# Token forms' hi copies moved behind, the output weights split earlier, and another order in the fold: one change to a fused attention and MLP kernel on one core

## The chip, the cores and the metric

The kernel runs on one core of a Trainium2 chip. The time is device time in microseconds (us) of one launch. The names in the profile: PE is TensorE's matmul, PEld its weight load, DVE VectorE, ACT ScalarE, POOL GpSimd, SP SyncE, whose queue issues nearly all DMAs. Each engine takes its instructions in the order in which they stand in its queue, and waits on semaphores where an operand or a buffer is not ready.

## The reference, cut to what matters

```python
def _A_ref(x, wqkv, w_phi, wo):                      # S=2048, D=640, H=32 heads of 20
    q, k, v = split_heads(x @ wqkv)
    pq, pk = einsum("bhsd,hdf->bhsf", q, w_phi), einsum("bhsd,hdf->bhsf", k, w_phi)
    phi_q = concat([softmax(pq), softmax(-pq)], -1)
    phi_k = concat([softmax(pk), softmax(-pk)], -1)
    kv, z = einsum("bhsf,bhsd->bhfd", phi_k, v), sum_s(phi_k)
    o = (phi_q @ kv) / (phi_q @ z + 1e-6)
    return merge_heads(o) @ wo
def _B_ref(x, w1, b1, w2, b2):                       # F=1728
    h = gelu(layernorm(x) @ w1 + b1)
    return h @ w2 + b2
xn = layernorm(x)
return x + _A_ref(xn, ...) + _B_ref(xn, ...)
```

All is float32. The kernel gets that precision from matmuls in a shorter format by splitting each operand exactly into a hi and a lo part: hi is a rounded copy (mostly on ACT), lo is the operand minus hi (on DVE or POOL). A product is then three matmuls, hi*hi, hi*lo and lo*hi (`mm3`).

## The kernel before, in words

The 2048 tokens are four blocks of 512 (b = 0 to 3), the 640 channels five chunks of 128 (c). The stages follow each other on TensorE:

1. **First MLP pass** (tokens of blocks 0 and 1). The 1728 hidden units are handled in pairs of chunks, g = 0 to 6. `Mlp.passes(g, b)` has two halves. The first makes the hidden values: for each of two chunks five groups of `mm3`, then gelu (L293, on ACT), hi (L60, ACT) and lo (L63, DVE). The second makes five output chunks (m) with two groups each, and DVE adds each to `acc` (L338). The second half of one pass stands on TensorE behind the first half of the next. The outputs use three PSUM banks in turn, so output m+3 cannot start until L338 has read output m.
2. **Attention features** (L1025, L1397, L1401 on TensorE): q, k and v for sixteen token tiles t, then softmax features on all engines, and the sums kv (L1138). Some products of pairs of tiles are done with seven block products in place of eight, which needs sums and differences of both operands: the forms.
3. **Second MLP pass** (blocks 2 and 3), with attention's second half beside it, then the output product with `wo`, in hi and lo parts that lie ready in the DRAM buffers `wo_dram`.

**What runs beside the first MLP pass.** A generator (`mlp.beside`) is advanced by one step at each tick. A tick is one `mm3` group on TensorE, three matmuls, and the order in which its steps and the pass's own instructions are written is the order in the queues of ACT, DVE and POOL. SP's queue is ordered by the scheduler. The generator is `prep()`, and beside it `turned_forms()`:

- `prep_fold`, the fold: products of `wqkv` and `w_phi` (L650 on TensorE), seven jobs of two units, ten ticks each. Each unit's product is split into hi (L738, ACT) and lo (L741, DVE), and its two PSUM banks are used again by the next job. Between them `more_stats` takes layernorm statistics of later tokens on DVE.
- `turned_forms`: forms of blocks 0 and 1. For block 1 ACT's own queue issues the stores (L932).
- The later tokens (blocks 2 and 3), driven by a list of events (tick, step). For each token tile (c, b): a load of `xq` from `xT`, `centred` (L797, POOL), `scaled` (L800, DVE), `hi` (L804, ACT), `lo` (L808, DVE) and two stores. For each pair of channel chunks, a cycle q: `form_sub`, four subtractions (L834, POOL); `form_hi`, two copies (L838, ACT); `form_lo` (L842, DVE) and their stores (L845). Then four `combine` subtractions (L820, POOL), each with its hi (L804), lo (L825) and a store of 512 KB (L826). Hi and lo of tiles and combinations lie in two buffers `t` in turn.
- Where the pass takes its next weights (`take`), two hi copies (L60, ACT) and two lo subtractions (L63, POOL) stand among these.
- At the end `raw_sums` prepares sums of the weights for attention's products. Steps that the ticks did not reach are written out in one go before g = 6's second pass.

**The order in attention** is found by a list scheduler at build time (`Plan.run`): each operation gets an assumed duration, times `LONGER` for all engines but TensorE, and each engine takes the operation that is due first. The rest follows in TensorE's order. The lo part of a k feature (L1090) goes to POOL or DVE, whichever the planner finds free. `plan_wo` puts the splitting of `wo` there: ten pieces of 128 x 320, from tile 4 on, each with a load (L1518, SP) into the buffer `r2`, a hi copy (L1521, ACT), a subtraction (L1524, POOL) and two stores (L1528). `r2` also holds weights of the second MLP pass, split there by L1550 (ACT) and L1551 (POOL). In the same queues v's hi and lo parts stand: L1119 (ACT) and L1124 (DVE). They free the PSUM bank of the projection.

Of the kernel before, what the change touches and what calls it, by code (L numbers as in the profile page):

```python
# [9 lines left out]
F32R = mybir.dt.float32r  # L10
AF = mybir.ActivationFunctionType
# [4 lines left out]
P = 128  # L16
S, D, F, H, DH = 2048, 640, 1728, 32, 20
KC = D // P
# [32 lines left out]
def tile_kernel(ctx: ExitStack, tc: tile.TileContext, x, xT, wkT, wqT, wv, wphi, wo, w1, b1, w2, b2,  # L51
# [671 lines left out]
    def prep_fold(batch, ts, done=None):  # L723
# [21 lines left out]
        for n, d in enumerate(done):  # L745
            yield from split_w(*d)
            for _ in range(3 + n):
                yield

    def more_stats():  # L750

        def tiles():
            xbs = {}
            for t in (*range(8, 16), None):
                if t is not None:
                    xbs[t] = gp.tile([P, 2, 512], F32, name="t").rearrange("p a c -> p (a c)")[:, :D]
                    with tc.issue_after(loads[1]):
                        nc.sync.dma_start(xbs[t], x[t * P:(t + 1) * P, :])
                if xbs and t != 8:
                    yield xbs.pop(min(xbs))  # L760
        yield from stats(range(8, 16), gp, tiles())
        for _ in range(2):
            yield
        yield from rows(2, 2, gp, mlp.px, 5)

    def prep():
        ahead = []
        more = more_stats()
        for i, job in enumerate(jobs):
            for k, _ in enumerate(prep_fold(job, ahead, None if i else first_done)):  # L770
                if k == 0 and i < 6:
                    ahead = raws(jobs[i + 1])
                if i > 0 and k % 3 == 1:
                    next(more, None)
                yield
# [72 lines left out]
        form_places = {2: temps[:4], 3: [z[:, o:o + 2 * P] for z in (spare[0], own["t"]) for o in (0, 2 * P)]}  # L848

        for n, step in enumerate(raw_sums(0, temps)):  # L850
            events.append((118 + 3 * n, len(events), step, ()))
        base = 8
        for q in range(3):
# [5 lines left out]
            if q < 2:  # L859
                for b, at, his, los in ((2, 14, (16, 18), (18, 20)), (3, 19, (21, 23), (23, 25))):  # L860
                    for i in range(4):
                        events.append((base + at + i, len(events), form_sub, (b, q, i)))
                    for i in range(2):
                        events.append((base + his[i], len(events), form_hi, (b, q, i)))
                        events.append((base + los[i], len(events), form_lo, (b, q, i)))
            base += 5 * len(tiles) + 5
            if q < 2:
# [42 lines left out]
    def turned_forms():  # L910

        for b, q in ((1, 1), (1, 0), (0, 0), (0, 1)):
# [9 lines left out]
            for i in range(2):  # L922
# [5 lines left out]
                yield 1  # L928
            yield 2
            for i, z in enumerate(parts):  # L930
# [3 lines left out]
            if (b, q) == (1, 0):  # L934
                yield 18

# [313 lines left out]

    LANDS, SOON, HURRY, AFTER, LONGER = 4.0, 0.9, -1.0, 10.0, 1.02
    plan = Plan()
# [125 lines left out]
    def plan_pair(t):  # L1378
# [70 lines left out]
        plan_wide(t, b1)  # L1449
        for n in range(t - 4, t - 2) if t > 2 else ():  # L1450
            plan_wo(n, at[t, 0])
        plan_kv(t - 1, c)
# [57 lines left out]
    def plan_wo(n, *after):  # L1510

        kc, cols = n // 2, slice(n % 2 * 320, n % 2 * 320 + 320)
        raw = {}

        def load():
            r = rp.tile([P, D], F32, name="r2")
            raw.update(lo=r[:, :320], hi=r[:, 320:])
            nc.sync.dma_start(raw["lo"], wo[kc * P:(kc + 1) * P, cols])  # L1518

# [6 lines left out]
        def store():  # L1526
            for w, wd in zip((raw["hi"], raw["lo"]), wo_dram):
                nc.sync.dma_start(wd[:, kc, cols], w)  # L1528

        a = plan.add("SP", 0.7, load, *after, *wo_done)  # L1530
        b = plan.add("ACT", 0.4, hi, a)
        c = plan.add("POOL", 1.0, lo, b)
        wo_done[:] = [plan.add("SP", 1.4, store, c)]
# [673 lines left out]
```

## Time and profile before

| | |
|---|---|
| median of 3 runs | 718.24 us (717.66 to 718.51) |
| the profiled execution | 718.39 us, span 716.6 us |
| busy PE, DVE, POOL, ACT | 97%, 77%, 71%, 53% of the span |
| first MLP pass | to about 224.7 us |
| attention features | 224.7 to 446.0 us |
| second MLP pass and output | from 446.0 us |
| mean granted TensorE clock | 0.99 |

A row of the timeline has the start in us, the duration, engine, line, operation, output<-input, shape and count. In brackets stands the idle time of that engine just before, and what released it. "SPq" and "ACTq" are DMA issues. The list of waits has, for each pair of waiter and releaser, the total, how many times, and the longest.

### The profile page before, as it was taken

What the parts mean: (1) busy time and instruction counts of PE and PEld (TensorE: products, weight loads), DVE (VectorE), ACT (ScalarE), POOL (GpSimd) and SP (SyncE); (2) the same over time, 40 slices, a digit from 0 to 9 for tenths busy, and PEclk for the clock granted to TensorE, in tenths of its full rate; (3) what the DMA queues carried; (4) which work ended last, traced back from release to release, by engine and by line L of the source; (5) the groups of instructions that cost most, each with busy time, mean ns of one, the idle gap of its engine ahead of it and who ended that gap; (6) DMA issues with size and microseconds to landing.
All of it is one profiled execution on the core that took longest, in us unless ns stands there. A gap on an engine that the chain in (4) does not pass through costs nothing.

```text
span 716.6 us, 9974 instructions
## 1 busy us (share of the span) xinstructions
PE 691.6 (97%) x3295; PEld 580.7 (81%) x3295; DVE 549.6 (77%) x915; ACT 376.8 (53%) x646; POOL 506.5 (71%) x389
## 2 busy tenths in 40 slices
PE   9999999788999999999999996999999999999998
PEld 7888888676788888888888784888888888888886
DVE  7869664777877889988989785958587687789783
ACT  6444744434433646545545353646667675659360
POOL 4707675749538678888888895868589988487940
PEclk9999999989999999999999998999999999999999
DMA  9816748567735014555553567485435548972112
GB/s 326 258 39 211 238 133 270 204 215 246 231 111 206 11 59 163 157 157 210 140 145 99 160 168 265 144 240 168 131 105 173 177 141 272 319 264 80 74 74 104
DMA packets 78299, 123.38 MB, mean 172 GB/s; under 512 B 8598, under 2 KB 43958, under 8 KB 75854
## 3 DMA queue, kind: packets, MB, share of 16 engines
q1 hardware_dynamic: 75766, 120.62, 52.9%
q10 hardware_dynamic: 2480, 2.11, 1.0%
q8 instruction: 26, 0.43, 0.2%
q14 instruction: 27, 0.22, 0.1%
HBM read 79.76 MB, written 42.94 MB: 171 GB/s over the span
## 4 chain that ended last, share of the span: by engine, by line
PE 77%; DVE 6%; POOL 6%; DMA 5%; issue 3%; ACT 2%; SPq 0%; POOLq 0%; DVEq 0%; ACTq 0%
PE bank L69 16%; PE bank L71 16%; PE bank L70 16%; PE bank L1025 11%; PE bank L1397 7%; DMA xq<-in_xT 2%; PE bank L1401 2%; PE bank L650 2%; PE bank L1138 2%; POOL m L1057 1%; PE bank L1748 1%; PE bank L1749 1%; POOL acc L834 1%; POOL xq L797 1%; DMA r<-in_wo 1%
## 5 line engine op out<-in xcount | busy, mean ns | idle before, releaser
L69 PE MATMUL bank<-m,w 128*128 128x512 f32 x288 | 114.0, 396 | 9.7 <-DVE acc L338 9.7
L70 PE MATMUL bank<-m,w 128*128 128x512 f32 x288 | 112.6, 391 | 0.0
L71 PE MATMUL bank<-m,w 128*128 128x512 f32 x266 | 104.1, 391 | 0.0
L69 PE MATMUL bank<-y,w 128*128 128x512 f32 (+1 forms) x256 | 99.6, 389 | 0.3 <-DVE v L1124 0.3
L70 PE MATMUL bank<-y,w 128*128 128x512 f32 (+1 forms) x256 | 98.8, 386 | 0.0
L71 PE MATMUL bank<-y,w 128*128 128x512 f32 (+1 forms) x246 | 95.0, 386 | 0.0
L63 POOL TENSOR_TENSOR w<-r,w 128x640 fp32r<-128x640 f32 x29 | 48.9, 1700 | 35.4 <-ACT w L60 30.7
L69 PEld LDWEIGHTS bank<-m,w 128*128 128x128 f32 x288 | 54.5, 189 | 22.4 <-DVE acc L338 11.0
L1025 PE MATMUL bank<-w,y 128*128 128x512 f32 x240 | 59.6, 401 | 8.1 <-DVE v L1124 8.1
L70 PEld LDWEIGHTS bank<-m,w 128*128 128x128 f32 x288 | 54.5, 189 | 11.0
L1025 PE MATMUL bank<-wkh,y 128*128 128x320 f32 (+1 forms) x240 | 63.1, 337 | 0.0
L1025 PEld LDWEIGHTS bank<-w,y 128*128 128x128 f32 x240 | 45.7, 193 | 17.7 <-DVE v L1124 6.6
L71 PEld LDWEIGHTS bank<-m,w 128*128 128x128 f32 x266 | 50.2, 189 | 10.7
L338 DVE TENSOR_TENSOR acc<-bank,acc 128x512 f32<-128x512 f32 x70 | 47.2, 683 | 13.9 <-PE bank L71 8.3
L69 PEld LDWEIGHTS bank<-y,w 128*128 128x128 f32 x256 | 48.1, 188 | 10.8 <-DVE v L1124 0.5
L1078 POOL TENSOR_TENSOR m<-m,w 128x1280 f32<-128x1280 f32 x16 | 43.4, 2712 | 18.6 <-DVE w L1071 14.7
L70 PEld LDWEIGHTS bank<-y,w 128*128 128x128 f32 x256 | 48.1, 188 | 9.4
L71 PEld LDWEIGHTS bank<-y,w 128*128 128x128 f32 x246 | 46.2, 188 | 9.4
L1057 POOL TENSOR_TENSOR m<-m,mx 128x640 f32<-128x640 f32 x32 | 40.9, 1279 | 15.0 <-DVE mx L1047 7.0
L1742 POOL TENSOR_TENSOR e<-e,m 128x512 fp32r<-128x512 f32 x28 | 41.0, 1467 | 14.8 <-ACT m L1741 11.9
L1065 DVE TENSOR_REDUCE sm<-m 128x64 f32<-128x1280 f32 x32 | 47.2, 1476 | 2.7 <-ACT m L1060 2.5
L1060 ACT ACTIVATE m<-m,rs_all 128x1280 f32<-128x1280 f32 x32 | 43.5, 1362 | 7.4 <-POOL m L1057 7.3
(307 smaller groups left out, 1794.2 us busy)
## 6 DMA issues: line engine op xcount, KB each, us to landing
r<-in_w SPq DMA_DIRECT2D x52, 320.0 KB
e<-e SPq DMA_DIRECT2D x40, 256.0 KB
e<-acc SPq DMA_DIRECT2D x52, 160.0 KB
w<-f SPq DMA_DIRECT2D x6, 1024.0 KB
t<-t SPq DMA_DIRECT2D x8, 512.0 KB
acc<-in_xT SPq DMA_DIRECT2D x3, 1280.0 KB
tf<-t SPq DMA_DIRECT2D x2, 1536.0 KB
xb<-in_x SPq DMA_DIRECT2D x8, 320.0 KB
```

The source lines that it names most:

```text
L63: eng.tensor_tensor(lo, src, f(hi), op=ALU.subtract)
L69: nc.tensor.matmul(ps, lh, rh, start=first, stop=False, **kw)
L70: nc.tensor.matmul(ps, lh, rl, start=False, stop=False, **kw)
L71: nc.tensor.matmul(ps, ll, rh, start=False, stop=last, **kw)
L338: nc.vector.tensor_tensor(acc[b][:, m, :], pw, acc[b][:, m, :], op=ALU.add)
L1025: nc.tensor.matmul(ps, lh[:, kc, c], rh[:, kc], start=n == 0, stop=n == 3 * KC - 1)
L1057: subs[n, t] = nc.gpsimd.tensor_tensor(ep[:, :, s], a, b, op=ALU.subtract)
L1060: exps[n, t] = nc.scalar.activation(e, e, AF.Exp, scale=rs_all[:, t:t + 1])
L1065: nc.vector.tensor_reduce(sm, e.rearrange("p a (h f) -> p (a h) f", f=DH), axis=AX, op=ALU.add)
L1078: nc.gpsimd.tensor_tensor(e3, e3, w.unsqueeze(2).to_broadcast([P, 2 * H, DH]), op=ALU.mult)
L1397: nc.tensor.matmul(ps, left(yn, pl, q), right(w, pr, q), start=first and q == 0 and n == 0, stop=False, skip_group_check=True)
L1742: mlp.after(1, lambda: nc.gpsimd.tensor_tensor(pl, e, f(ph), op=ALU.subtract))
```

## The change

Three things, the parts of the diff in the order of the program:

1. The fold: in `prep_fold` the second unit's hi and lo come one tick earlier in the job's ten, and the statistics are advanced at steps 2, 5 and 8 of a job and not at 1, 4 and 7. `more_stats` begins one step later. In `turned_forms` the four stores of form (1, 0), which ACT issues, come six ticks later, and the pause behind them is six shorter.
2. The forms of the later tokens: `form_hi` stands 9 ticks (block 2) and 8 ticks (block 3) later behind its subtractions, `form_lo` with it; the cycles of q = 0 and 1 become four ticks longer each, and `raw_sums` is four ticks later.
3. `wo`: columns 0 to 511 of all five chunks are loaded, split and stored by new events of the first MLP pass (`wo_load`, `wo_hi` 8 ticks later, `wo_lo` 2 ticks after that), in the buffers in which the forms of the same cycle are made. `plan_wo` keeps columns 512 to 639, in three pieces at tiles 2, 4 and 6. `LONGER` is 1.04, it was 1.02.

```diff
@@ prep_fold, more_stats, prep
-            for _ in range(3 + n):
+            for _ in range(2 + 3 * n):
                 yield
...
+        yield
         yield from stats(range(8, 16), gp, tiles())
...
-                if i > 0 and k % 3 == 1:
+                if i > 0 and k % 3 == 2:
                     next(more, None)
@@ events of the later tokens
+        wos = {}
+        def wo_load(kc):
+            wos[kc] = [(temps[0], temps[1]), (temps[2], temps[3]), (spare[0], own["t"])][kc % 3]
+            nc.sync.dma_start(wos[kc][0], wo[kc * P:(kc + 1) * P, :512])
+        def wo_hi(kc):
+            nc.scalar.activation(wos[kc][1].bitcast(F32R), wos[kc][0], AF.Copy)
+        def wo_lo(kc):
+            nc.gpsimd.tensor_tensor(wos[kc][0].bitcast(F32R), wos[kc][0], wos[kc][1], op=ALU.subtract)
+            for w, wd in zip(wos[kc][::-1], wo_dram):
+                nc.sync.dma_start(wd[:, kc, :512], w)
+        for kc, at in enumerate((46, 49, 52, 97, 100)):
+            for after, step in ((0, wo_load), (8, wo_hi), (10, wo_lo)):
+                events.append((at + after, len(events), step, (kc,)))
         for n, step in enumerate(raw_sums(0, temps)):
-            events.append((118 + 3 * n, len(events), step, ()))
+            events.append((122 + 3 * n, len(events), step, ()))
...
-                for b, at, his, los in ((2, 14, (16, 18), (18, 20)), (3, 19, (21, 23), (23, 25))):
+                for b, at, his, los in ((2, 14, (25, 27), (27, 29)), (3, 19, (29, 31), (31, 33))):
...
-            base += 5 * len(tiles) + 5
+            base += 5 * len(tiles) + (9 if q < 2 else 5)
@@ turned_forms
-            yield 2
+            yield 8 if (b, q) == (1, 0) else 2
...
-                yield 18
+                yield 12
@@ the planner
-    LANDS, SOON, HURRY, AFTER, LONGER = 4.0, 0.9, -1.0, 10.0, 1.02
+    LANDS, SOON, HURRY, AFTER, LONGER = 4.0, 0.9, -1.0, 10.0, 1.04
...
-        for n in range(t - 4, t - 2) if t > 2 else ():
-            plan_wo(n, at[t, 0])
+        if t < 8:
+            plan_wo(t // 2 - 1, at[t, 2])
@@ plan_wo
-        kc, cols = n // 2, slice(n % 2 * 320, n % 2 * 320 + 320)
+        ks, cols = slice(2 * n, min(2 * n + 2, KC)), slice(512, D)
...
-        c = plan.add("POOL", 1.0, lo, b)
+        c = plan.add("POOL", 0.7, lo, b)
```

TensorE's order stays as it was, but for one small transpose. Where the order moves on the other engines (line numbers behind the event list are up to 20 higher in the new file: L804 is L805, L838 is L839, L1119 is L1138, L1550 is L1570):

ACT in the first cycle of the later tokens, before (L293 and L60 with a bank are the two gelus of a pass, L804 hi copies, L838 the forms' hi copies, L60 with w the next weights):

```order
L804 ACTIVATE t<-xq 128x512
L838 ACTIVATE acc_1300<-acc_1300 128x512 x2
L293 ACTIVATE bank_1433<-bank_1433,b1t 128x512
L60 ACTIVATE m_1432<-bank_1433 128x512
L804 ACTIVATE t<-xq 128x512
L838 ACTIVATE s_1301<-acc_1300 128x256 x2
L293 ACTIVATE bank_1469<-bank_1469,b1t 128x512
L60 ACTIVATE m_1468<-bank_1469 128x512
L804 ACTIVATE t<-xq 128x512 x2
```

and after the change:

```order
L805 ACTIVATE t<-xq 128x512
L293 ACTIVATE bank_1433<-bank_1433,b1t 128x512
L60 ACTIVATE m_1432<-bank_1433 128x512
L805 ACTIVATE t<-xq 128x512
L293 ACTIVATE bank_1464<-bank_1464,b1t 128x512
L60 ACTIVATE m_1463<-bank_1464 128x512
L839 ACTIVATE acc_1300<-acc_1300 128x512 x2
L839 ACTIVATE s_1301<-acc_1300 128x256 x2
L805 ACTIVATE t<-xq 128x512
```

Two of the forms' hi copies stood ahead of each gelu; now both gelus come first.

SP behind the first cycle's forms, before (L845 stores of forms, L826 of combinations, L794 loads of later tokens, L251 and L252 of weights):

```order
L845 DMA f_95<-s_1301 128x256
L810 DMA yl_77<-t 128x512
L845 DMA f_95<-acc_1300 128x256 x2
L826 DMA t_86<-t 128x1024
L794 DMA xq<-in_xT 128x512
L826 DMA t_86<-t 128x1024
L251 DMA r_1562<-in_w 128x640
```

and after it (L855 loads of `wo`):

```order
L846 DMA f_95<-s_1301 128x256
L855 DMA acc_1300<-in_wo 128x512
L846 DMA f_94<-acc_1300 128x2x256
L846 DMA f_95<-acc_1300 128x256
L855 DMA acc_1300<-in_wo 128x512
L846 DMA f_95<-acc_1300 128x256
L827 DMA t_86<-t 128x1024
L251 DMA r_1557<-in_w 128x640
L827 DMA t_86<-t 128x1024
L795 DMA xq<-in_xT 128x512
```

Two loads of `wo` now stand among the stores of the forms whose buffers they reuse, and ahead of the stores of the combinations.

ACT at the end of attention, before (L1550 weights of the second MLP pass, L1521 a piece of `wo`, L1119 hi of v):

```order
L1550 ACTIVATE w_4038<-r_4030 128x640
L1521 ACTIVATE r_4060<-r_4060 128x320
L1119 ACTIVATE v_2180<-bank_4092,rs_all 128x11x12
L1037 ACTIVATE m_2187<-bank_4092 128x32x6
L1087 ACTIVATE w_4149<-m_4062 128x1280
L1119 ACTIVATE v_2180<-bank_4119,rs_all 128x10x48
L1119 ACTIVATE v_2180<-bank_4119,rs_all 128x32
L1060 ACTIVATE m_4146<-m_4146,rs_all 128x1280
L1119 ACTIVATE v_2183<-bank_4151,rs_all 128x11x12
L1037 ACTIVATE m_2187<-bank_4151 128x32x6
L1119 ACTIVATE v_2183<-bank_4175,rs_all 128x10x48
```

and after it:

```order
L1570 ACTIVATE w_4029<-r_4021 128x640
L1138 ACTIVATE v_2205<-bank_4080,rs_all 128x11x12
L1056 ACTIVATE m_2212<-bank_4080 128x32x6
L1106 ACTIVATE w_4135<-m_4051 128x1280
L1138 ACTIVATE v_2205<-bank_4107,rs_all 128x10x48
L1138 ACTIVATE v_2205<-bank_4107,rs_all 128x32
L1079 ACTIVATE m_4132<-m_4132,rs_all 128x1280
L1138 ACTIVATE v_2208<-bank_4137,rs_all 128x11x12
L1056 ACTIVATE m_2212<-bank_4137 128x32x6
L60 ACTIVATE w_4221<-r_4185 128x640
L1138 ACTIVATE v_2208<-bank_4161,rs_all 128x10x48
```

The piece of `wo` is gone from here, and a split of second-pass weights (L60) stands ahead of the last hi part of v; it stood behind the first gelus of the second pass before.

More of the change, by code (lines that the diff above doesn't have):

```diff
@@ L1516, in load @@
             r = rp.tile([P, D], F32, name="r2")
-            raw.update(lo=r[:, :320], hi=r[:, 320:])
-            nc.sync.dma_start(raw["lo"], wo[kc * P:(kc + 1) * P, cols])
+            w = (ks.stop - ks.start) * P
+            raw.update(lo=r[:, :w], hi=r[:, 320:320 + w])
+            nc.sync.dma_start(raw["lo"].rearrange("p (c n) -> p c n", n=P), wo[ks.start * P:ks.stop * P, cols].rearrange("(c p) n -> p c n", p=P))
         def hi():
@@ L1527, in store @@
             for w, wd in zip((raw["hi"], raw["lo"]), wo_dram):
-                nc.sync.dma_start(wd[:, kc, cols], w)
+                nc.sync.dma_start(wd[:, ks, cols], w.rearrange("p (c n) -> p c n", n=P))
         a = plan.add("SP", 0.7, load, *after, *wo_done)
         b = plan.add("ACT", 0.4, hi, a)
-        c = plan.add("POOL", 1.0, lo, b)
+        c = plan.add("POOL", 0.7, lo, b)
         wo_done[:] = [plan.add("SP", 1.4, store, c)]
```

## Prediction

> **What bounds the kernel now.** I read the page first, then TensorE's waits, then its timeline at each wait, and last the other three engines at the same moments.
>
> ```profile
> PE 691.6 (97%) x3295; PEld 580.7 (81%) x3295; DVE 549.6 (77%) x915; ACT 376.8 (53%) x646; POOL 506.5 (71%) x389
> ...
> PE bank L69 <- DVE acc L338: 9.7, 3, 6.3
> PE bank L1025 <- DVE v L1124: 8.1, 2, 6.3
> PE bank L650 <- PE bank L650: 1.5, 2, 0.9
> ```
>
> TensorE is busy 97% of a span of 716.6 us, and the diff adds and removes no matmul. So only waiting can be won: these three groups (total, times, longest) hold 19.3 us. Where they lie, and what a wait costs beyond itself:
>
> ```profile
> 139.22 0.39 PE L71 MATMUL bank<-m,w 128*128 128x512 f32 x1
> 145.86 0.79 PE L69 MATMUL bank<-m,w 128*128 128x512 f32 x1 [6.25 <-DVE acc L338]
> 146.45 0.63 PE L70 MATMUL bank<-m,w 128*128 128x512 f32 x1
> 148.99 0.39 PE L70 MATMUL bank<-m,w 128*128 128x512 f32 x1
> 177.94 0.50 PE L69 MATMUL bank<-m,w 128*128 128x512 f32 x1 [3.13 <-DVE acc L338]
> 178.28 0.40 PE L70 MATMUL bank<-m,w 128*128 128x512 f32 x1
> 179.95 0.50 PE L69 MATMUL bank<-m,w 128*128 128x512 f32 x1 [0.36 <-DVE acc L338]
> 404.51 2.78 PE L1025 MATMUL bank<-w,y 128*128 128x512 f32 x11 [1.75 <-DVE v L1124]
> 426.39 3.59 PE L1025 MATMUL bank<-w,y 128*128 128x512 f32 x15
> 438.51 5.57 PE L1025 MATMUL bank<-w,y 128*128 128x512 f32 x15 [6.33 <-DVE v L1124]
> ```
>
> After the 6.25 us wait the next seven matmuls take 148.99 - 145.86 = 3.13 us. Normal spacing is (3.59 - 0.39) / 14 = 0.23 us, so seven take 1.6: 1.5 us lost at half clock. Fifteen matmuls after the 6.33 us wait take 5.57 instead of 3.59: 2.0 us. After 3.13 and 1.75 us nothing of this is seen. So the waits cost 6.25 + 1.5 = 7.8 (first), 3.13 + 0.36 = 3.5 (second), 1.5 (the fold's), 1.75 and 6.33 + 2.0 = 8.3 (late attention): 22.9 us.
>
> **First cycle of the token forms (7.8 us).** What stood ahead of the accumulation L338 that freed the bank:
>
> ```profile
> 128.84 3.83 POOL L63 TENSOR_TENSOR w<-r,w 128x640 fp32r<-128x640 f32 x2 [3.21 <-ACT w L60]
> 138.18 0.88 POOL L834 TENSOR_TENSOR acc<-xq 128x128 f32<-128x128 f32 x2
> 139.03 0.99 POOL L834 TENSOR_TENSOR acc<-xq,acc 128x128 f32<-128x128 f32 x2
> 135.78 0.63 ACT L838 ACTIVATE acc<-acc 128x512 fp32r<-128x512 f32 x1 [3.83 <-POOL acc L834]
> 138.25 0.63 ACT L838 ACTIVATE acc<-acc 128x512 fp32r<-128x512 f32 x1 [1.84 <-POOL acc L834]
> 138.79 0.64 ACT L293 ACTIVATE bank<-bank,b1t 128x512 f32<-128x512 f32 x1
> 139.46 0.60 ACT L60 ACTIVATE m<-bank 128x512 fp32r<-128x512 f32 x1
> 135.08 1.21 DVE L800 TENSOR_TENSOR xq<-xq,m 128x512 f32<-128x512 f32 x1 [1.87 <-POOL xq L797]
> 140.09 0.69 DVE L63 TENSOR_TENSOR m<-bank,m 128x512 fp32r<-128x512 f32 x1 [2.47 <-ACT m L60]
> 145.13 1.88 DVE L338 TENSOR_TENSOR acc<-bank,acc 128x512 f32<-128x512 f32 x3
> ```
>
> POOL was late with the form subtractions (L834). ACT stood on them with the hi copies (L838), the gelu L293 behind them. DVE stood on that gelu's lo part (L63), and then had 5 us of queue before L338. In the new order both of the pass's gelus stand ahead of all four hi copies. Step by step, with POOL unchanged up to here: L800 ends at 136.3; the token tile's hi copy (0.63, as L838) at 136.9; gelu and its copy (0.64 + 0.60) at 138.2; L63 (0.69) at 138.9; the first L338 (1.88 / 3 = 0.6) at 139.5, and the matmul that waits for it is due at 139.45. The first wait falls to 0.1. The form's lo parts then follow one by one between accumulations, when POOL has been done since 140.0.
>
> What is late next is the combined forms' chain: two buffers t, each freed only when its 512 KB store has landed.
>
> ```profile
> 152.63 0.32 SPq L826 DMA_DIRECT2D t<-t  x1
> 156.23 0.63 ACT L804 ACTIVATE t<-xq 128x512 fp32r<-128x512 f32 x1 [1.17 <-DMA t<-t]
> 139.00:182.00 43.00, 33.26 (x138) 26.44 (x137) 32.33 (x41) 19.26 (x34) 29.25 (x26) 0.92 0.69 229
> ```
>
> The first two rows: 3.6 us from issue to release. The matmul at 139.22 ends tick 156, so tick t is due at 139.45 + 0.68 (t - 156): the third combined hi copy (tick 167) at 146.9, the gelu of tick 170 behind it at 149.0. SP, in order, now meets the first load of wo among the forms' stores, and must wait there until one of them has landed. The first combined store, ready near 144 (POOL's first two subtractions from 140.0, then hi and lo), should go out near 145 and land 4 to 5 us later. That gives hi copy 150.6, gelu 151.9, L63 152.6, L338 153.2, against a matmul due at 153.0 (end of tick 176); the next accumulation is about 1 us late behind the fourth lo part. So 1.5 us of new waiting; bounds 0 (out at 144, landing after 3.6) and 4.
>
> **Second cycle (3.5 us), with three pieces of wo ahead of it.** Each piece adds one ACT copy, one POOL subtraction and three DMAs of 256 KB, which share this stretch.
>
> ```profile
> L820 POOL TENSOR_TENSOR xq<-xq x8: 1273/1452/1742, 140.0 to 187.1; 128x512 f32<-128x512 f32 x8
> L800 DVE TENSOR_TENSOR xq<-xq,m x10: 677/1210/2051, 122.7 to 199.5; 128x512 f32<-128x512 f32 x10
> ```
>
> POOL: three of the nearest shape, 3 x 1.45 = 4.4 us. Its busy time in the quoted 43 us (last row of the fence before; columns: window, its length, busy TensorE, weight load, DVE, ACT, POOL, clock, DMA share, GB/s) is 29.3, and without about 11 us of waiting the stretch is 32 us, plus 8 ticks (5.4 us) that the change puts into the two cycles: 33.7 in 37, tight. POOL runs some 4 us behind at the second set of subtractions, as before. The gelu again stands ahead of the hi copies, but the last token tile's L800 stands ahead of the second accumulation and still waits for POOL. I keep 1.5 us of the 3.5; bounds 0 and 4.
>
> DMA: 229 GB/s over 43 us are 9.8 MB. Put into 37 us with 9 x 0.26 = 2.4 MB more, that is 330 GB/s, where a share of 0.69 now gives 229, so 332 when full. This stretch becomes nearly DMA-bound, and I add 1.0 us for it (bounds 0 and 5). ACT's copies (0.63 each) lie in its idle time (43 - 19.3). The last two pieces come at ticks 224 to 229, where TensorE, by the rows above, has no wait until 404, and cost nothing; if that cover went, 2 x 1.45 of POOL. Eight more ticks push the last token tile's split behind the end of the cycle pass, to where raw_sums is already dumped: 0.
>
> First pass: 7.8 + 3.5 less 0.1 + 1.5 + 1.5 + 1.0 = 4.1, a gain of 7.2.
>
> [...]
>
> **The fold (1.5 us).** The second unit's hi and lo parts come one tick earlier, ahead of the statistics on DVE.
>
> ```profile
> 81.75 1.12 DVE L741 TENSOR_TENSOR wkl<-bank,wkh 128x156 fp32r<-128x156 f32 x4 [0.20 <-ACT wkh L738]
> 82.98 1.12 PE L650 MATMUL bank<-wpt,raw 120*128 120x114 f32 x8 [0.88 <-PE bank L650]
> 79.54 0.66 ACT L293 ACTIVATE bank<-bank,b1t 128x512 f32<-128x512 f32 x1 [4.91 <-DMA t<-in_x]
> ```
>
> The product at 82.98 follows the end of L741 (82.9). One tick is 0.68: the two waits of 0.88 and 0.63 keep 0.2. But ACT's 4.91 us behind its own stores of the b=1 forms is what made L741 late; those stores move 6 ticks and may block elsewhere. Gain 1.0; bounds -1 and 1.5.
>
> **Late attention (1.75 + 8.3 us).**
>
> ```profile
> 402.26 0.47 ACT L1521 ACTIVATE r<-r 128x320 fp32r<-128x320 f32 x1 [5.73 <-DMA r<-in_wo]
> 432.42 1.53 POOL L1551 TENSOR_TENSOR w<-r,w 128x640 fp32r<-128x640 f32 x1
> 433.98 0.35 SPq L1518 DMA_DIRECT2D r<-in_wo  x1
> 437.10 0.47 ACT L1521 ACTIVATE r<-r 128x320 fp32r<-128x320 f32 x1 [10.56 <-issue]
> 438.10 0.36 DVE L1124 SCALAR_TENSOR_TENSOR v<-bank,rs_all,v 128x132 fp32r<-128x132 f32 x1 [9.22 <-ACT m L1037]
> ```
>
> Both waits are ACT standing on a wo copy whose load had not landed; the last load could not start until POOL's L1551 gave the buffer r2 back. In the new order the last wo copy is far earlier, and none stands here, so L1119 and L1124 run as soon as the projection ends. Late next is a split that moves up (L60 of w2's second half, ahead of the last v copy): it needs a load after L1551. L1551 also ends earlier (ACT no longer holds up POOL's products at 402, and two wo subtractions go), so I put 0.8 us there; bounds 0 and 4. Gain 10.0 - 0.8 = 9.2.
>
> **Attention's order (225 to 380).** The planner's factor 1.04 changes which of POOL and DVE takes some lo parts (L1090), and reorders DVE.
>
> ```profile
> 225.00:380.00 155.00, 155.00 (x800) 134.51 (x799) 136.26 (x225) 78.21 (x126) 126.25 (x95) 1.00 0.44 137
> ```
>
> TensorE never waits here now; nothing can be won. DVE gives work to POOL, whose 126 us leave room. Cost 0.3; bounds 0 and 3.
>
> **Sum.** 7.2 + 1.0 + 9.2 - 0.3 = 17.1 us. The profiled execution took 718.39 us beside its span of 716.6, 0.15 above the median of 718.24. 718.39 - 17.1 = 701.3; I say 701.
>
> **Rivals.**
> A. The forecast, 696 to 706: chance 0.70.
> B. The first pass gives its gain back: DMA near full, POOL 4 us behind, and L800 or the fourth lo part holds L338 again. For it: shares 0.69 and 29.3 us above. Against: the hi copies no longer hold the gelu. All 11.3 us stay, 718.39 - 1.0 - 9.2 + 0.3 = 708.5. Chance 0.13. [...]
> C. A new wait in attention or its end (the moved split, the new order) of about 5 us: 706. Chance 0.10.
> D. Slower: wo_hi stands on its load as L1521 did, in both groups of pieces. ACT holds the gelu, as it held L1119: 10.56 us on ACT cost 8.3. It decides when each of the five copies waits over 6 us: five times 5.73 is 28.7 us on ACT, and with nothing to hide it the time is 718.39 - 17.1 + 28.7 - 8 (the ticks ahead of each group) = 722. Against it: 8 ticks (5.4 us) between load and copy. Chance 0.04.
> E. The waits only move and nothing measurable changes (718): 0.03.
>
> Low 695.5: all 22.9 us gone. High 710 takes in B and C; D and E stay out. 0.2% (1.4 us) is about what can be told from no change: faster 0.93, same 0.03, slower 0.04.
>
> **What would show it.** TensorE's waits after: L69 on L338 under 5 us in total, none over 3; L1025 on L1124 under 1.5; L650 under 0.5; no copy of a wo piece with over 3 us of idle before it. Clock near 1.00 around 140 and 435. It is wrong if the accumulation wait returns near 150 to 170, or if the moved L60 shows a long wait on r.

## The result, and the profile after

The changed kernel takes 707.84 us (median of 4 runs, 706.7 to 709.4) against 718.38 (717.66 to 720.13) of the kernel before beside it: a ratio of 0.9851, 95% interval 0.9825 to 0.9877. The profiled execution took 707.67 us with a span of 705.9; the span is 10.7 us shorter. The forecast of faster holds and 707.8 lies in the range (695.5 to 710), but outside the 696 to 706 to which I had given 0.70; the likeliest value was 701, and 6.4 of the 17.1 us that I expected did not come.

TensorE's line on the page after, and then its waits (total, times, longest):

```profile
PE 691.2 (98%) x3295; PEld 579.6 (82%) x3295; DVE 544.3 (77%) x912; ACT 376.6 (53%) x644; POOL 516.1 (73%) x390
```

```profile
PE bank L69 <- DVE acc L338: 3.7, 4, 2.6
PE bank L314 <- DVE w L63: 3.4, 1, 3.4
...
PE bank L71 <- POOL w L63: 1.2, 1, 1.2
```

Two of the three old groups are gone: nothing waits at the fold (L650) or in the narrow projection (L1025, now L1044). The accumulation group is 3.7 us in four pieces. Two groups are new, both for the lo part of a weight (L63). Where they lie, from TensorE's timeline:

```profile
152.43 0.50 PE L69 MATMUL bank<-m,w 128*128 128x512 f32 x1 [0.22 <-DVE acc L338]
154.67 0.50 PE L69 MATMUL bank<-m,w 128*128 128x512 f32 x1 [0.59 <-DVE acc L338]
161.48 0.50 PE L71 MATMUL bank<-y,w 128*128 128x512 f32 x1 [1.18 <-POOL w L63]
171.43 0.50 PE L69 MATMUL bank<-m,w 128*128 128x512 f32 x1 [2.63 <-DVE acc L338]
194.87 0.79 PE L314 MATMUL bank<-y,w 128*128 128x512 f32 x1 [3.41 <-DVE w L63]
```

The 6.25 us wait of the first cycle is gone, and everything from 150 us on is new. Waits alone don't give the balance, since half clock comes on top (0.50 from 193.79 to 200.62, rows at the end). So I compare the two traces matmul by matmul: both hold 3295 in the same order (one transpose aside), and the difference of the start times of the n-th is what has been won up to there. The change of that difference in each stage, in us (plus is won), with stages given in the time of before:

| stage | predicted | changed kernel | forms' delay alone | the transfers added to that |
|---|---|---|---|---|
| start to 82 | 0 | -0.8 | -0.1 | -0.1 |
| 82 to 94, fold | +1.0 | +2.0 | +1.0 | +1.0 |
| 94 to 150, first cycle's wait | +7.7 | +7.8 | +8.0 | +7.4 |
| 150 to 183, combined forms, second cycle | -0.5 | -1.8 | +1.4 | -4.1 |
| 183 to 221, end of the cycle pass | 0 | -7.6 | -1.7 | -7.7 |
| 221 to 402, attention | -0.3 | +0.2 | -0.1 | 0.0 |
| 402 to 449, late attention | +9.2 | +11.4 | 0.0 | -0.2 |

The second column less the first is the miss: 8.9 us too little between 150 and 221, 3.0 more elsewhere. (The last two columns are two of the experiments below; after 449 us the changed kernel keeps its 11.2 to within 0.5.) Late attention is clean. The windows of before, then of after (columns: window, its length, busy TensorE, weight load, DVE, ACT, POOL, each with its count, clock, DMA share, GB/s):

```profile
400.00:420.00 20.00, 18.25 (x94) 15.49 (x94) 17.19 (x25) 11.76 (x18) 17.18 (x13) 1.00 0.63 155
420.00:440.00 20.00, 13.67 (x74) 12.00 (x73) 9.03 (x18) 6.64 (x14) 13.24 (x11) 0.89 0.50 138
```

```profile
400.00:420.00 20.00, 20.00 (x104) 17.23 (x103) 18.74 (x28) 11.88 (x17) 17.33 (x14) 1.00 0.59 134
420.00:440.00 20.00, 20.00 (x111) 17.62 (x111) 17.12 (x27) 12.40 (x19) 19.36 (x14) 1.00 0.37 110
```

TensorE is busy for all 40 us at full clock, where it idled 8.1 before.

What holds L314 near 195: ACT's rows of after, then SP's.

```profile
189.11 0.63 ACT L805 ACTIVATE t<-xq 128x512 fp32r<-128x512 f32 x1 [6.00 <-DMA t<-t]
193.30 0.63 ACT L805 ACTIVATE t<-xq 128x512 fp32r<-128x512 f32 x1 [3.56 <-DMA t<-t]
193.84 0.45 ACT L60 ACTIVATE w<-r 128x320 fp32r<-128x320 f32 x1
```

```profile
182.32 0.40 SPq L855 DMA_DIRECT2D acc<-in_wo  x1
...
183.78 0.44 SPq L827 DMA_DIRECT2D t<-t  x1
...
184.78 0.97 SPq L855 DMA_DIRECT2D acc<-in_wo  x1
187.97 0.33 SPq L966 DMA_DIRECT2D acc<-in_wv  x1
188.39 0.38 SPq L827 DMA_DIRECT2D t<-t  x1
```

The last weight tile's split (L60 at 193.84) stands on ACT behind the hi parts of the third and fourth combined form, and each of these stands on the landing of a 512 KB store t<-t. The first store goes out at 183.78 between two loads of wo, the pieces that I had costed at nothing, and releases its buffer at 189.11: 5.3 us. The split comes behind the second landing, 193.30, and there SP's own order counts too. The lo part of that second combination ends at 185.18 (DVE's row), but its store leaves only at 188.39: a load of `wv` (L966, 187.97) stands ahead of it, and SP waited for that until a store of a form had landed (SP's wait).

```profile
184.50 0.68 DVE L826 TENSOR_TENSOR t<-xq,t 128x512 fp32r<-128x512 f32 x1
```

```profile
SPq L966 <- DMA f<-acc: 2.2, 1, 2.2
```

It is the chain that I had named for the first cycle, at work in the second, in front of a weight split that I had not looked at.

### The profile page after: what moved, and what is told of

Its sections match the earlier page's. It is cut to its first block, busy times and chain, and to the rows that moved or that the text cites. A ratio compares the mean times of both kernels' runs of the same rounds, so it can differ in the third digit from the quotient of the medians.

```text
span 705.9 us, 9957 instructions
## 1 busy us (share of the span) xinstructions
PE 691.2 (98%) x3295; PEld 579.6 (82%) x3295; DVE 544.3 (77%) x912; ACT 376.6 (53%) x644; POOL 516.1 (73%) x390
## 4 chain that ended last, share of the span: by engine, by line
PE 82%; DVE 6%; DMA 5%; POOL 3%; issue 2%; ACT 2%; SPq 0%; DVEq 0%; POOLq 0%; ACTq 0%
PE bank L1044 17%; PE bank L69 15%; PE bank L71 15%; PE bank L70 15%; PE bank L1416 8%; PE bank L1157 3%; PE bank L1420 2%; PE bank L650 2%; POOL xq L798 1%; PE bank L1768 1%; PE bank L1769 1%; DMA t<-t 1%; DMA f<-xq 1%; PE bank L556 1%; DVE acc L843 1%
## 5 line engine op out<-in xcount | busy, mean ns | idle before, releaser
L69 PE MATMUL bank<-m,w 128*128 128x512 f32 x288 | 113.9, 396 | 3.7 <-DVE acc L338 3.7
L71 PE MATMUL bank<-m,w 128*128 128x512 f32 x266 | 103.8, 390 | 0.0
L69 PE MATMUL bank<-y,w 128*128 128x512 f32 (+1 forms) x256 | 99.6, 389 | 0.0
L71 PE MATMUL bank<-y,w 128*128 128x512 f32 (+1 forms) x246 | 95.1, 387 | 1.2 <-POOL w L63 1.2
L63 POOL TENSOR_TENSOR w<-r,w 128x640 fp32r<-128x640 f32 x29 | 49.5, 1719 | 30.2 <-ACT w L60 25.6
L69 PEld LDWEIGHTS bank<-m,w 128*128 128x128 f32 x288 | 54.4, 189 | 17.3 <-DVE acc L338 5.7
L1044 PE MATMUL bank<-wkh,y 128*128 128x320 f32 (+1 forms) x240 | 63.1, 337 | 0.0
L71 PEld LDWEIGHTS bank<-m,w 128*128 128x128 f32 x266 | 50.1, 188 | 10.7
L1044 PE MATMUL bank<-w,y 128*128 128x512 f32 x240 | 57.5, 391 | 0.0
L69 PEld LDWEIGHTS bank<-y,w 128*128 128x128 f32 x256 | 48.1, 188 | 10.4 <-ACT bank L1836 0.3
L71 PEld LDWEIGHTS bank<-y,w 128*128 128x128 f32 x246 | 46.2, 188 | 11.1 <-POOL w L63 1.6
L338 DVE TENSOR_TENSOR acc<-bank,acc 128x512 f32<-128x512 f32 x70 | 46.4, 680 | 8.5 <-PE bank L334 5.0
L1044 PEld LDWEIGHTS bank<-w,y 128*128 128x128 f32 x240 | 44.4, 188 | 8.5
L1097 POOL TENSOR_TENSOR m<-m,w 128x1280 f32<-128x1280 f32 x16 | 41.3, 2584 | 11.3 <-DVE w L1090 10.0
L1138 ACT ACTIVATE v<-bank,rs_all 128x132 fp32r<-128x132 f32 (+2 forms) x48 | 19.6, 443 | 52.4 <-PE bank L1044 52.1
```

The source lines that it names most:

```text
L63: eng.tensor_tensor(lo, src, f(hi), op=ALU.subtract)
L69: nc.tensor.matmul(ps, lh, rh, start=first, stop=False, **kw)
L71: nc.tensor.matmul(ps, ll, rh, start=False, stop=last, **kw)
L338: nc.vector.tensor_tensor(acc[b][:, m, :], pw, acc[b][:, m, :], op=ALU.add)
L1044: nc.tensor.matmul(ps, lh[:, kc, c], rh[:, kc], start=n == 0, stop=n == 3 * KC - 1)
L1097: nc.gpsimd.tensor_tensor(e3, e3, w.unsqueeze(2).to_broadcast([P, 2 * H, DH]), op=ALU.mult)
```

## Experiments

Every kernel was timed in rounds beside the kernel before; ratios are to that, since its median differs between the sets of runs (718.4 to 720.9 us).

**Which part loses the first pass.** delay_only is before with

```diff
-for b, at, his, los in ((2, 14, (16, 18), (18, 20)), (3, 19, (21, 23), (23, 25))):
+for b, at, his, los in ((2, 14, (25, 27), (27, 29)), (3, 19, (29, 31), (31, 33))):
-base += 5 * len(tiles) + 5
+base += 5 * len(tiles) + (9 if q < 2 else 5)
```

and raw_sums at 122; wo_only is before with the five pieces of wo (ticks 42, 45, 48, 89, 92) and the three pieces in attention.

> The kernel before with one part of the change: the forms' hi and lo parts 8 ticks further behind their subtractions, both cycles moved to suit. No piece of wo in the first pass, fold and late attention as before. Counted matmul by matmul in the two traces, the whole change is worth 8.8 us at the first wait, but between 146 and 220 us it loses all of that again: 0.8 at two short accumulation waits, 1.6 at a wait for a weight's lo part, 2.6 at the accumulation near 171 (before: 3.5), 6.2 at the matmul L314 near 195 (3.4 of waiting and 2.8 at half clock), 1.2 after it. Theory D (the delay itself does it: it brings the last combined forms in front of the last weight's split on ACT): the wait at L314 is here too, about 3 us and half clock, and the time is 718.4 - 8.8 - 3.5 + 6.2 = about 712. Theory P (the three pieces of wo do it, by their nine transfers and their POOL steps): no wait over 1 us between 150 and 220, and the time is 718.4 - 8.8 - 3.5 + 1 = about 707.

> The kernel before with one part of the change: the first 512 columns of wo are split in the first pass (at ticks 42, 45, 48, 89, 92, as far behind the undelayed forms as in the change), the rest in three pieces in attention; forms and fold as before. Late attention gains the 10 to 11 us that it gains in the whole change. Theory D: the pieces lie between the cycles and cost nothing much: waits of 7.8 and 3.5 us as before, time 718.4 - 10.5 = 708. Theory P: between 146 and 220 us 5 to 9 us more are waited than before, time 713 to 717.

delay_only: 711.79 us, 0.9878 (0.9853 to 0.9903). wo_only: 713.46, 0.9905 (0.9888 to 0.9923). By the table the delay alone wins 7.7 us between 94 and 221 (8.0 + 1.4 - 1.7), nearly the 7.2 that I gave the whole first pass; the whole change wins -1.6 there. So the pieces of wo cost 9 us. The wait at L314 does exist without them, but at a third of its size and with no half clock (1.00 from 190 to 200):

```profile
PE bank L69 <- DVE acc L338: 1.4, 2, 0.9
...
PE bank L314 <- DVE w L63: 1.1, 1, 1.1
```

The times alone don't decide. Both theories reckoned from a before of 718.4, and 0.9878 of that is 709.6, between D's 712 and P's 707 (711.8 looks like D's number only because its own before took 720.9). The waits do: D's wait at L314 explains 1.1 us, and the rest comes with the pieces, as P said. wo_only lost 3.4 us between 150 and 183, part of it a second stretch of half clock from 178 (0.75 from 180 to 190), and 0.7 from there to 221; it won 10.9 in late attention. Its loss of 4.1 lies a little under the 5 to 9 of theory P, and its time, 0.9905 of 718.4 or 711.6, between D's 708 and P's 713.

**Steps or transfers.** no_early_sub leaves out POOL's subtraction for the first three pieces, so its lo parts are the plain load; bytes_only is delay_only with the fifteen transfers of the pieces and none of their ACT or POOL steps.

```diff
 # no_early_sub, in wo_lo
-    nc.gpsimd.tensor_tensor(...)
+    if kc > 2:
+        nc.gpsimd.tensor_tensor(...)
 # bytes_only, on delay_only
+for kc, at in enumerate((46, 49, 52, 97, 100)):
+    for after, step in ((0, wo_load), (10, wo_store)):   # two stores of the plain load
```

> The changed kernel without the three POOL subtractions of the first pieces of wo (their lo part is then the plain load; loads, hi copies and stores stay). Theory Q: POOL's forms and combined subtractions of the second cycle run 3 to 3.8 us earlier, the wait for a weight's lo part (1.2 near 161) goes, the accumulation wait near 171 falls from 2.6 to under 1, the wait at L314 falls to 1 or less (chain 3 us earlier, TensorE 2.9 us earlier, so 3.3 if it only shifts): time 3 us lower, 6 if the half clock goes too. Theory S: the early waits go, but L314 waits 3.4 us as before, because the store still needs 5.3 us: time about 3 us lower at most.

> The kernel of delay_only with the fifteen transfers of the five pieces of wo at their places in the first pass (five loads of 256 KB, and ten stores of the plain load to where attention writes the split parts later), without their five ACT copies and five POOL subtractions; wo is still split in attention as before. Matmul by matmul, the first pass gained 7.6 us in delay_only and lost 1.4 in the changed kernel. Theory B (the bytes: 15 x 0.26 = 3.9 MB more through DMA engines that are 0.95 to 1.03 busy between 150 and 160 us and again near 185): waits of 0.5 to 2 us between 150 and 172, 3 to 4 near 195 with half clock behind, first pass about 0, time 711.8 + 7 to 9 = 719 to 721 on that chip's scale (0.997 to 1.0 of the kernel before). Rival (the copies and subtractions on ACT and POOL do it): as delay_only, 0.988.

bytes_only: 721.79 us, 1.0029 (1.0010 to 1.0049), 0.3% slower than before, where delay_only was 1.2% faster. Its loss from 150 to 221 is 11.8 us (4.1 + 7.7) against 0.3 in delay_only; about 3.0 of it is lost to a stretch of half clock, 163.7 to 170.5 with 6.07 us of TensorE work, that the profiled run of the changed kernel doesn't have. (The ratios put bytes_only 10.9 us behind delay_only: 0.0151 of 720.) The waits at L314 and L71 are those of the changed kernel, somewhat longer; of the accumulation waits only one near 154 is left, and a wait of 1.4 for a weight's hi part is new near 162:

```profile
PE bank L314 <- DVE w L63: 4.7, 1, 4.7
PE bank L69 <- DVE acc L338: 1.5, 1, 1.5
PE bank L71 <- POOL w L63: 1.4, 1, 1.4
```

no_early_sub: 707.43 us, 0.9825 (0.9804 to 0.9847), not to be told from the unaltered kernel (0.9841 beside it), and -9.4 from 150 to 221 as in the table (1.7 of it half clock from 163.0). Theory Q fell on the time: POOL, without its three subtractions, simply waits for the next tile of x. Its rows in no_early_sub, then in the changed kernel:

```profile
154.79 1.29 POOL L798 TENSOR_TENSOR xq<-xq,m 128x512 f32<-128x512 f32 x1 [5.91 <-DMA xq<-in_xT]
177.62 6.39 POOL L821 TENSOR_TENSOR xq<-xq 128x512 f32<-128x512 f32 x4
```

```profile
155.13 1.30 POOL L798 TENSOR_TENSOR xq<-xq,m 128x512 f32<-128x512 f32 x1
178.14 6.38 POOL L821 TENSOR_TENSOR xq<-xq 128x512 f32<-128x512 f32 x4
```

In no_early_sub the x tile lands at 154.8, so a free POOL can begin no sooner, and the second set of subtractions starts only half a microsecond earlier.

One part of theory Q did come true: nothing waits near 171 in no_early_sub (nor in bytes_only). In the changed kernel that wait of 2.63 does stand on POOL, which has no idle over 0.6 us from 153.9 to 176. Its third subtraction for a piece (L861) stands ahead of the x tile on which, one after the other, `scaled` on DVE, a hi copy on ACT and the gelu behind it depend:

```profile
163.36 1.30 POOL L861 TENSOR_TENSOR acc<-acc,s 128x512 fp32r<-128x512 f32 x1
164.60 1.75 POOL L798 TENSOR_TENSOR xq<-xq,m 128x512 f32<-128x512 f32 x1
166.39 1.22 DVE L801 TENSOR_TENSOR xq<-xq,m 128x512 f32<-128x512 f32 x1 [1.19 <-POOL xq L798]
167.63 0.63 ACT L805 ACTIVATE t<-xq 128x512 fp32r<-128x512 f32 x1 [3.77 <-DVE xq L801]
```

With the subtractions gone, other waits take its place: 1.03 at 153.2 and 0.57 at 160.2, and the half clock. So two limits lie close together. The transfers alone bring the whole loss; POOL's steps on top of them add nothing that shows (1.2 us, intervals overlapping). What the steps would cost without the transfers was not run. And bytes_only adds, with the bytes, fifteen places in SP's queue and the waits for the buffers; for the first stretch, 150 to 176, these are not parted from the bytes.

How full the DMA engines are where it hurts, from windows of the changed kernel:

```profile
150.00:160.00 10.00, 9.19 (x39) 6.71 (x37) 7.31 (x11) 5.07 (x9) 5.90 (x5) 1.00 1.03 352
190.38:193.79 3.41, 1.07 (x5) 0.56 (x3) 1.28 (x3) 0.49 (x1) 1.28 (x1) 1.00 1.02 403
```

Full (share 1.03 and 1.02), twice: while the first combined stores, three pieces and the next x tiles share them, and again under the second combined stores. But the first spell is nearly as full in delay_only, where TensorE loses nothing in it. Two windows of delay_only, then the second of them in the changed kernel:

```profile
150.00:160.00 10.00, 9.33 (x40) 6.93 (x38) 7.04 (x11) 4.42 (x8) 5.01 (x3) 1.00 0.97 335
160.00:170.00 10.00, 9.12 (x40) 7.11 (x39) 6.96 (x9) 3.93 (x7) 9.92 (x11) 1.00 0.52 172
```

```profile
160.00:170.00 10.00, 7.62 (x33) 5.74 (x31) 5.01 (x6) 3.71 (x7) 10.00 (x8) 1.00 0.84 314
```

What the pieces add to a full spell runs on behind it, and the landings in it come later: the stores t<-t of the first cycle on which ACT stands take 3.0, 6.0 and 4.8 us from issue to release in delay_only, and 4.4, 7.5 and 6.8 in bytes_only.

**Which transfers, and which order.** hold_loads keeps the last two loads of wo behind the second store t<-t on SP's queue; last_form_late lets the fourth combined form come after the weight's split; wo_late puts all five pieces behind the second cycle.

```diff
 # hold_loads
+with tc.issue_after(stored[5].ins) if kc > 2 else ExitStack():
     nc.sync.dma_start(wos[kc][0], wo[kc * P:(kc + 1) * P, :512])
 # last_form_late
+wait = 8 * (q == 1 and n == 3)
-... (3, hi ...), (5, combined_lo)
+... (3 + wait, hi ...), (5 + wait, combined_lo)
 # wo_late: two pairs of buffers, raw_sums at 143
-for kc, at in enumerate((46, 49, 52, 97, 100)):
+for kc, at in enumerate((95, 98, 110, 113, 125)):
```

> The changed kernel, but on SP's queue the loads of the last two pieces of wo stand behind the second store t<-t of the second cycle instead of around the first. Theory S (those two loads share the DMA engines with that store: its way from issue to release took 5.3 us in the changed kernel, 3.0 with the delay alone, and the last hi part, then the weight's split, then L314 stand on it): release after 3.0 to 3.5 us, wait at L314 from 3.4 to about 1.2, no half clock there, time 5 us under the changed kernel's. Theory Q (the three POOL subtractions of the first pieces push everything 3.1 us back, and the loads don't matter): wait at L314 stays over 3, time within 1 us of it.

> The changed kernel, but the hi and lo parts of the fourth combined form of the second cycle come 8 ticks later, so that on ACT the split of the last weight tile stands ahead of that hi part and no longer behind the landing of its buffer's store. If that wait is what costs 3.4 us and, by the half clock, 2.8 more: no wait at L314, clock 1.00 from 190 to 205, time 707.8 - 6.2 = 701.6. Rival (the chain is only shifted: the third hi part, the gelu behind or POOL's next step holds TensorE instead): a wait of 2 to 4 us elsewhere between 190 and 220, time 705 to 708.

> The changed kernel, but all five pieces of wo come after the second cycle (ticks 95, 98, 110, 113, 125, two pairs of buffers in turn, the sums of weights 21 ticks later), where the DMA engines were 0.27 to 0.43 busy. Theory D: the wait at L314 stays (2 to 3.5 us and half clock), the short waits before it go: 707.8 - 1.6 - 1 = 705. Theory P: all of it goes: 707.8 - 6.2 - 1.6 - 1.8 - 1.2 = 697 to 698.

> The changed kernel unaltered, as the measure for the three runs beside it: by its earlier ratio 0.985 of the kernel before. Waits of 1.2 near 161, 2.6 near 171 and 3.4 near 195 us, as earlier; half clock after the last, or after the one near 171, since last_form_late showed half clock for 3.4 us after a wait of 2.6 there.

changed_again, the measure beside hold_loads: 708.62 us, 0.9841 (0.9822 to 0.9860), with the waits expected (1.2, 2.6 and 3.8 us) and half clock after the last two. hold_loads: 706.97, 0.9821 (0.9802 to 0.9840); the intervals overlap. ACT's and SP's rows in it:

```profile
186.07 0.63 ACT L805 ACTIVATE t<-xq 128x512 fp32r<-128x512 f32 x1 [3.69 <-DMA t<-t]
191.64 0.63 ACT L805 ACTIVATE t<-xq 128x512 fp32r<-128x512 f32 x1 [4.94 <-DMA t<-t]
```

```profile
182.72 0.41 SPq L827 DMA_DIRECT2D t<-t  x1
...
184.99 0.38 SPq L827 DMA_DIRECT2D t<-t  x1
185.42 1.62 SPq L856 DMA_DIRECT2D acc<-in_wo  x2
```

Theory S was right on the store, 3.35 us (182.72 to 186.07) in place of 5.3, and wrong on the time: the two loads now share the engines with the second store, which takes 6.65 (184.99 to 191.64; 5.5 in delay_only, without the loads). L314 still waits 2.5 us. Moving the loads by one store moves the wait by one store.

last_form_late: 705.44 us, 0.9789 (0.9771 to 0.9806). The loss from 183 to 221 is 3.7 in place of 7.6 to 8.0: the place of the wait is confirmed, at two thirds of its predicted price. The split now stands behind the third hi part only,

```profile
190.42 0.63 ACT L805 ACTIVATE t<-xq 128x512 fp32r<-128x512 f32 x1 [5.70 <-DMA t<-t]
190.95 0.46 ACT L60 ACTIVATE w<-r 128x320 fp32r<-128x320 f32 x1
```

and L314 still waits 1.0 us, but at full clock; an accumulation wait of 1.0 is new near 214.

wo_late was worse than the change, 716.45 us, 0.9939 (0.9919 to 0.9959), and a bad design of mine. The wait at L314 stayed (4.3 us), because SP still issued the first two loads around the combined stores, ahead of the ticks at which their steps stand; and the sums of weights, due before the pass ends, had to wait for the last store of a piece, with L338 queued behind them on DVE. DVE's row, then TensorE's:

```profile
218.42 0.69 DVE L918 TENSOR_TENSOR acc<-wkh,wkl 128x512 f32<-128x512 f32 x1 [9.78 <-DMA wol<-acc]
```

```profile
223.83 0.80 PE L69 MATMUL bank<-m,w 128*128 128x512 f32 x1 [10.50 <-DVE acc L338]
```

So its time tells nothing on P against D, only that this pass has no room for the pieces behind the cycles either. Its stages tell more. Without the three early pieces, 150 to 183 is back at +1.5 us, as in delay_only (+1.4; -1.8 in the changed kernel), so these three cost 3.3 there. And two loads of `wo` at the combined stores, with no piece before them, are enough for a wait of 4.3 at L314 where delay_only has 1.1.

**Putting it together.** all_three joins hold_loads and last_form_late and takes two early pieces' hi and lo parts sooner (46 + 4 and 47 + 4 in place of + 8). wo_sooner takes the other way out: the delay and the fold's order, no piece of wo in the first pass, and attention's ten pieces earlier in the plan:

```diff
-for n in range(t - 4, t - 2) if t > 2 else ():
+for n in range(t - 2, t) if t < 12 else ():
     plan_wo(n, at[t, 0])
```

wo_sooner_form_late adds last_form_late to it.

> The changed kernel with three edits: the last two loads of wo held back as in hold_loads; the fourth combined form of the second cycle 8 ticks later as in last_form_late; and the hi and lo parts of the first two pieces of wo 4 to 6 ticks earlier, so that two of POOL's three subtractions lie in the 4.9 us that it idles before 153.9. If S and Q each carry their part: waits near 161 and 171 fall to under 0.5 and 1.5, none at L314, time 718.4 - 17 = 701 on the first chip's scale, 0.976 of the kernel before. Rival: the earlier hi copies of wo stand on their loads ahead of a gelu, as in a copy of wo before; then a new accumulation wait of 1 to 3 us near 150, and 704 (0.980).

> The kernel before with the delay of the forms and the new order of the fold, no piece of wo in the first pass; the ten pieces of attention start one pair of tiles earlier in the plan (range(t - 2, t) for t up to 10, in place of range(t - 4, t - 2)). If the pieces' place in the first pass is what cost 9 us, and late attention waited only because its last two loads (408 and 434 us before) came too late: first pass +7.6, fold +1.8, late attention +8 to 10, time 0.974 to 0.976 of the kernel before (about 701 to 703 where that takes 720). Rival (the r buffers: pieces that come sooner make a weight load or a copy on ACT wait elsewhere): a wait of 2 to 7 us between 240 and 440, 0.980 to 0.988.

> wo_sooner, and the fourth combined form of the second cycle 8 ticks later as in last_form_late. The wait of 1.1 us at L314 that delay_only keeps should go: 1 us under wo_sooner. Rival: L314 then stands on the third combined hi part instead and nothing changes, within 0.5 us of wo_sooner.

all_three: 703.67 us, 0.9775 (0.9751 to 0.9800). Both named cases came: no wait at L314, and a new accumulation wait of 1.5 at 153.7. The waits near 161 and 171 did not fall as expected (0.8 and 2.2, the latter with half clock behind it). wo_sooner: 702.53, 0.9767 (0.9737 to 0.9797). wo_sooner_form_late: 700.88 beside 719.57, 0.9744 (0.9713 to 0.9775), the lowest of all, though its interval overlaps that of wo_sooner, and not a piece of wo in the first pass. The wait at L314 is gone, as expected. Its page and its waits:

```profile
PE 688.4 (99%) x3295; PEld 577.8 (83%) x3295; DVE 550.0 (79%) x915; ACT 377.1 (54%) x646; POOL 510.4 (73%) x389
```

```profile
PE bank L69 <- DVE acc L338: 2.5, 3, 1.6
PE bank L1027 <- DVE v L1126: 1.7, 1, 1.7
```

Late attention wins 9.5 us there (11.4 in the change; the 1.7 us wait near 395 is left), the first pass 8.0 from 94 to 221 (7.6 + 0.7 - 0.3) in place of the change's -1.6; 1.3 is lost after 449. The late wait wanted the last loads of wo earlier; it did not want them in the first pass.

## Why the prediction was right, and where it was not

- **First cycle, right.** Predicted 7.7 us, measured 7.8 and, with the delay alone, 8.0. The order of hi parts and gelus on ACT was the cause.
- **Combined forms' chain.** 1.5 us predicted near 150 to 155; 0.22 + 0.59 came. Its mechanism, a hi part that stands on the landing of a store t<-t, came back in the second cycle with 5.3 us a landing, where I had not priced it.
- **The steps that failed: the DMA term and the pieces at "cost nothing".** I had worked out 330 GB/s of 332 for the stretch and added 1.0 us (bounds 0 and 5), a figure worked out from nothing; I had said that the last two pieces cost nothing; and that the eight ticks of delay at the pass's end cost 0. Together with the second cycle's terms this made -0.5 us from 150 to 221. The delay alone gave -0.3, as predicted. With the pieces it was -9.4, and the transfers alone give -11.8. So the transfers were to be priced at 9 us, not 1. It was not the mean that misled: it said full, while from 139 to 176 the changed kernel moved 288 GB/s at a share of 0.83. What I didn't do was follow the chains through the spells that are full (1.03 and 1.02), where stores on which ACT stands land later and what stands behind them on ACT and SP waits too.
- **Half clock.** 2.9 us of the 9 are half clock after the wait at L314 (from 194.87 to 200.62, half of 5.75; rows below), for which the sum had no term.
- **Second accumulation wait.** I kept 1.5; 2.63 is there, 0.9 in delay_only, and none without the three subtractions. So it is POOL and the tile of x behind it, as I had put it, and too small by 1.1; but with the subtractions gone the transfers hold TensorE elsewhere for as long.
- **Fold, right.** Predicted 1.0. The pair shows 2.0, but the kernels with the old fold also start 1.0 earlier there than the profiled run of before, so the edit is worth the 1.0 between them.
- **Late attention, too low.** Predicted 9.2, measured 11.4: 10.0 of waits and half clock as I had them, about 1.4 in small gaps beside them, and no residual; the moved split waits for nothing that holds TensorE.
- **Attention's order.** Predicted -0.3, measured +0.2: free.
- **The rivals.** The time, 707.84, is rival B's (708.5, at 0.13). Its first reason, DMA engines near full, is what the runs show (1.03 and 1.02); its second, POOL, holds one wait (near 171) and not the time: with its three subtractions left out the time changed by 1.2 us, with overlapping intervals. That the time came within 7 us of my 701 is partly luck: late attention's extra 2.2 offsets a part of the loss in the first pass.
- **The signs that I named.** L69 on L338 under 5 us with none over 3, L650 gone, the narrow projection's waits gone, no wo copy after a long wait (1.3 us at most): all as listed. The list had no line for a weight split, so L314 passed it unseen.

## What to carry to other kernels

Price added transfers by the fullest spell that they fall into, and by the chains through it: here the spell was at 0.97 without them (150 to 160, delay_only), and with them (bytes_only) the stores on which ACT's queue stood took 4.4, 7.5 and 6.8 us in place of 3.0, 6.0 and 4.8. When two limits lie close together, taking one away shows nothing in the time, so look at the waits too. When a chain is moved later, list what stands behind its last member on each engine, down to the weight split of the end of the pass. And when two edits of one change win in different places, try them apart: here the better answer to the late wait was to start the old transfers sooner: it wins 2 us less there and doesn't cost the 9 in the first pass.

## What the hardware showed that I had not expected

From the waits of before (3.13; 6.25 and 6.33) I had taken it that a wait of 3.1 us keeps full clock and one of over 6 does not. The same 2.6 us wait near 171 us had no price in the changed kernel and one in its repetition. The windows of the first, then of the second:

```profile
168.20:171.60 3.40, 0.77 (x4) 0.35 (x3) 2.12 (x4) 1.21 (x3) 3.32 (x5) 1.00 0.21 78
171.60:175.02 3.42, 3.42 (x16) 2.79 (x17) 3.29 (x6) 2.37 (x4) 2.80 (x5) 1.00 0.67 235
```

```profile
168.24:171.66 3.42, 0.80 (x4) 0.36 (x3) 2.26 (x4) 1.10 (x2) 3.34 (x5) 1.00 0.25 92
171.66:175.07 3.41, 3.41 (x9) 2.65 (x8) 2.72 (x5) 1.15 (x2) 2.27 (x4) 0.50 0.68 239
```

Nine matmul starts in the second window in place of sixteen: 1.7 us. Stretches of half clock in all these runs, those at the very end aside, last 3.41 (171.66 to 175.07, above), 6.83 (before, 142.13 to 148.95) or 10.24 us (wo_late, up to 227.8), whole multiples of 3.41, and in the changed kernel the stretch after L314 is two of them:

```profile
193.79:197.20 3.41, 2.33 (x5) 1.79 (x6) 2.64 (x6) 2.79 (x6) 0.00 (x0) 0.50 0.31 118
197.20:200.62 3.42, 3.42 (x9) 2.67 (x9) 1.33 (x3) 0.59 (x1) 0.00 (x0) 0.50 0.38 153
200.62:204.03 3.41, 3.41 (x16) 2.79 (x15) 2.74 (x5) 2.40 (x4) 1.42 (x2) 1.00 0.08 28
```

So in these traces it matters where a wait falls on a grid of 3.41 us: a window with 0.80 us of work (168.24) or 1.07 (190.38, above) was followed by half clock, while the first kernel's equal wait (168.8 to 171.4) lay across a border of its grid (193.79 less seven times 3.41 is 169.9), with 2.31 and 1.89 us of work in the windows on its two sides, and cost nothing more. Laid on each trace's own grid, the thirteen traces agree (the first and last few us left out): every full-clock window with 1.49 us of TensorE work or less was followed by half clock (the 1.49 is in no_early_sub, at 159.59), and none with 1.56 or more (the 1.56 is in wo_only, at 137.23). The grid lies elsewhere in each execution: the borders 193.79 in the first and 171.66 in the second are 6.48 steps apart. The phase of the grid alone makes the 1.7 us above between two executions of one kernel.
